# Turning Q, K and u by TensorE in all pairs and half batches instead of by the DMA crossbar

## The chip, the core and the metric

The kernel runs on one core of one Trainium2 chip. The metric is the device time of one execution in microseconds (us), and the figure given is the median of three runs. The five engines are TensorE (PE; its weight loads are listed apart as PEld), VectorE (DVE), ScalarE (ACT), GpSimd (POOL) and SyncE (SP). Each runs its own list of instructions in order, and they meet only at semaphores.

## The reference

The inputs are q, k and v for 4 batches, 8 heads, 768 positions and 64 channels per head. Block-sparse attention is followed by a mixer with four weight matrices:

```python
scores = scale * np.matmul(q, k.transpose(0, 1, 3, 2))
# blocks of 32: neighbours, first and last block, 3 sampled blocks per query block
scores = np.where(mask, scores, -1000000000.0)
scores = scores - np.max(scores, axis=-1, keepdims=True)
attn = np.exp(scores)
attn = attn / (np.sum(attn, axis=-1, keepdims=True) + 1e-09)
x = np.matmul(attn, v)                  # per head; then (B, S, H * D) = (4, 768, 512)
h = np.maximum(xt @ w_tok1, 0.0) @ w_tok2          # xt: (B, 512, 768); 768 -> 256 -> 768
u = x + h.transpose(0, 2, 1)
h2 = np.maximum(u @ w_ch1, 0.0) @ w_ch2            # 512 -> 1536 -> 512
return u + h2
```

All inner products run in bf16 with sums in float32; the output is float32.

## The kernel before

Two heads make a pair; there are 16 pairs (NP), four to a batch. Positions are spread over the 128 partitions in steps of six, so a head's 768 positions are six chunks (NC) of 128. A pair goes through these steps:

- Q, K and V are loaded by GpSimd's DMA queue (load_pair, L457), V is copied beside a column of ones (relayout, L790), and for pairs from 4 on Q and K are copied into the tiles klay and qlay, where one chunk holds both heads (relayout, L793).
- K and Q are turned, so that channels stand on the partitions: ktb and qtb, four buffers each (NV). This is the function transposes. Pairs 1 to 7 do it on TensorE against the identity (L882) with a copy out of PSUM (L895 or L911). Pairs from NPE = 8 on call crossbar, in which SP issues a DMA transpose each for K and for Q (L816).
- Scores (L941) are made in nine steps for a pair: three blocks t of 256 queries by three blocks jj of 256 keys. From pair 4 on the two heads use the two 64-row halves of the array at once. ScalarE takes the exp (L953), and from pair 4 on VectorE multiplies with a 0/1 mask (L970).
- P times V goes through L1082 (full height, 65 columns) for the first 18 blocks of queries, and from there on through the helper halves, whose matmuls all carry L386: a sum over 128 rows is cut into two sums over 64, which run side by side in the two halves of the array and end in two banks. VectorE divides by the sum (L1038 and L1039, or L1095 and L1096) and writes x.

When four pairs are done, the mixer of that batch begins. Its token part works on half batches (b, g), 256 channels each: tok for batches 1 to 3, tok_first on quarters for batch 0. It adds the result to x in place; this is u. Then u has to be turned for the channel part, into the tile uT, whose channels lie in four blocks of 128 (2 g + m). Batch 0 does this in turn_first (L1427), half batch (1, 1) in turn_by_pe (L1161, with copies L1172), and the other five, (1, 0), (2, 0), (2, 1), (3, 0) and (3, 1), in turn_by_crossbar (L1141, a DMA transpose from SP). The channel part ch multiplies with w_ch1 (L386 in halves, L1528 at full height for the last batch), takes the ReLU (L1124 on ScalarE, L1126 on VectorE), multiplies with w_ch2 (L386, L1593), adds u (L1559, L1607, L1615) and stores.

turn_by_pe and the half-height branch of transposes are built alike: six chunks, each with two matmuls of 64 rows by 64 columns, one per half of the array, in transpose mode, so 12 for one operand of a pair or one block of uT. The result fills two of the eight PSUM banks, and one copy of 128 x 768 by VectorE or ScalarE brings it to SBUF.

The order of the work is written out by hand at the top, as the dictionary ORDER: one string per engine, in which a letter names a stream and a number repeats it. On TensorE q is a score step, v and V are P times V, t the transposes of K and Q, f and g the token part of batch 0, k and K that of the others, c and C the channel part (capitals are the second halves), s and m the start. On ScalarE and VectorE e is an exp, x a masking, n a division, l and y the copies of Q, K and V, h the copy of turned K or Q, w that of turned u, r a ReLU, o an output. On SP b and u are the crossbar transfers. The class Planner follows these strings step by step with a cost for each operation, chooses PSUM banks and buffers by its own clock and emits the instructions. Its costs (RING, CLASH and the numbers at each P.op) decide banks and buffers, not the order.

The event all_loaded keeps the copies of K and Q for pairs from NPE on, and so their crossbar transfers, back until the last input load has landed. Between the first and second half of a sum in halves stands a fence: a no-op at L372 on SP, or on GpSimd once its loads are issued, for which the second half waits.

Of the kernel before, what the change touches and what calls it, by code (L numbers as in the profile page):

```python
# [28 lines left out]
def spell(text):  # L29

    steps = []
    for word in text.split():
# [7 lines left out]
        s q s q s t q s t3 q t2 q t v s v t v q t4 q v q2 v m v q2 v3 t3 q t3 q v q v t f2 t f6 t2 f4 t q v  # L40
        q2 t v2 q v2 f12 q t9 q f3 v f q v f t2 f t q t5 f t f q f8 q f2 q2 t5 v2 q v f2 v3 t f q f3 v q f4
        t2 f t f q v2 q f2 t2 f2 t f2 q2 v f v f t v f2 q f3 t2 f3 t q t2 f2 q v t v2 t q v3 t4 f q t6 g12
        q2 f5 g6 t f5 t5 f g6 q2 t f t4 v f t f4 g6 q v2 c3 q c3 q c2 C2 q C6 q v6 c5 q c5 q c C c q C7 q C4
        c6 q c2 C2 q C c4 q C6 c C c C2 c q v9 c q2 C2 k6 C2 K2 c3 q K c K3 q C4 v3 k v5 k v k2 c2 v2 c v K4
        c k V k c4 K V4 K V3 C4 V2 C q C2 V2 C c6 q v2 c2 v c q c v c v2 c q v6 C2 V4 q C V2 C V4 q C3 V2 C
        q C4 c q c3 q c2 q v2 c v3 c v c v c q v c v4 c q V6 C3 V v2 V v3 V v5 V2 v2 V C v3 C v V5 v V2 v2
        V2 v3 V3 v2 q C3 V12 C3 c v c q v2 C c v c2 v8 c q V12 c q c3 q k6 c q K c K5 q C2 v12 k3 V12 k q K4
        k2 C2 K2 q C2 q C2 k C k11 C3 c3 v2 c q v5 C3 v5 C c V c v2 V4 v c V c V2 v4 V2 v V2 v4 q C V12 C q
        C2 c5 q c5 C q c C2 q C5 c v12 C2 V5 q V C V5 C V c4 q c4 C c q c C c2 C v7 C v3 C v2 C2 q C V C V3
        C V8 C c C c3 v q v11 C2 V12 q C2 c2 q c2 k4 C k2 q C3 K2 v3 K v2 K v7 K2 c2 V c V11 c q c k4 c2 q c  # L50
        K4 C q C7 c3 k2 c q K c K q c4 q v2 c v8 c v2 q c V12 C q C3 v5 q v2 C2 v5 C q V2 C V9 q V C4 q c3 q
        c3 v q c v c2 v c v q v6 c v2 c v8 V4 C v2 V3 v4 C V4 v3 V4 v2 V C V2 v V2 v2 V3 v2 V C2 q V7 C V q
        V4 C5 k2 q k C k3 v12 K6 V5 q c2 V2 c V2 k3 V k V2 c k K4 k c2 q c K2 c3 q c2 q2 C5 q C7 q v24 V24 q
        c2 q c4 q C2 c C2 v12 c q V12 C2 q C2 q c10 C c v2 C2 v2 q c C3 v2 C v C2 v4 C v C2 V4 v V2 v V2 v V
        v3 V3 v6 q V12 q c3 q k6 c v4 K6 q C3 v8 C k4 V12 K q K3 c3 q c5 q C2 k2 C2 q K2 C4 c4 v12 q C V9 v
        V v V2 C v C2 v5 c2 v4 q c2 V10 q V2 C3 q C c10 C c q C4 c q C2 c2 C c2 q c3 v c v5 q v C2 v q v4 C3
        v V3 v2 V2 v V C V v4 V2 v2 V3 v2 c5 V v V C2 v c V c V3 v V v3 V2 v2 c V v V2 v3 C3 V12 c2 C c2 k12
        c4 k12 c6 C12 c194
    """),
    act=spell("""  # L60
        p e38 ag e2 h e6 r e r e4 r e3 r e3 r e3 r e13 l e8 w e r e6 r e2 r e r e2 l e2 r e3 r e14 l e11 r
        e4 r2 e4 r e4 r e3 r e6 ak
    """),
    dve=spell("""
        Z3 Y z5 H2 z n H2 Y S n m n H2 af Y n H2 n df2 H2 L2 n wf h H2 af l Y n h df n y df n h l wf n l Y h
        af l n l n x h l h df dg df dg x h wf wg n x4 n2 x3 r y x y x r x n3 x2 ak y r dk2 x n y x3 n x o l2
        x3 n l y x n2 x o l n x2 l ak x n dk2 x w x o x l2 n l n r x2 r n x4 n x y n r l x2 ak n l dk x2 dk
        x l n x3 n l o x2 y x n2 x n x o ak x n dk2 x l y x y x o n2 x3 n r x3 n2 x2 ak x n dk x dk x2 n r x
        n y x r x3 n x n2 o dk3 r o r13 o r2 o2 r o3 r o3
    """),  # L70
    sp=spell("""
        s2 b3 u b11 u b u b u2
# [39 lines left out]
RING = {"b": (1170.0, 1200.0, 1100.0), "u": (1170.0, 2200.0, 1400.0)}  # L112
CLASH = 3500.0
# [192 lines left out]
def kernel(  # L306
# [23 lines left out]
    NPE = 8  # L330
# [447 lines left out]
    copied, LAYS = {}, {}  # L778
    all_loaded = Ev()

    def relayout(p):
        lays = LAYS[p] = {}
        for nm in ("k", "q", "v") if p >= NT0 else ("v",):
# [3 lines left out]
            def emit(eng, nm=nm, raw=raw):  # L787
                copy = nc.scalar.copy if eng == "act" else nc.vector.tensor_copy
                if nm == "v":
                    copy(out=vaug[p % NV][:, :, :, 0:64], in_=raw)  # L790
                else:
                    lay = sbw.tile([128, NC, 2, D], BF16, tag=f"{nm}lay", bufs=2, name=f"{nm}lay{p}")
                    copy(  # L793
                        out=lay[:, :, :, :], in_=raw.rearrange("p h c d -> p c h d")
                    )
                    lays[nm] = lay
# [6 lines left out]
            if nm != "v" and p >= NPE:  # L803
                deps.append(all_loaded)
            lays[nm + "ev"] = P.op(("dve", "act") if p >= FORM["relay_act"] else ("dve",), {"dve": 290.0, "act": 660.0}, deps, emit,
# [5 lines left out]
    def crossbar(p):  # L811

        lays = LAYS[p]
        for nm, bufs, there in (("k", ktb, kT_there), ("q", qtb, qT_there)):
            def emit(eng, nm=nm, bufs=bufs):
                nc.sync.dma_start_transpose(  # L816
                    out=bufs[p % NV][:, 0, :].rearrange("e (c s) -> e c s", c=NC),
                    in_=lays[nm][:, :, :, :].rearrange("p c h d -> p (c h d)"),
                )
            deps = [lays[nm + "ev"], qk_done[p - NV]]  # L820
            ev = P.op(("sp",), {"sp": 1300.0}, deps, emit, lat=3500.0, label="b")
# [3 lines left out]
    def transposes(p):  # L825
        yield lambda: p in LAYS
        if p >= NPE:
            crossbar(p)
            return
# [88 lines left out]
    def alias(a, b):  # L918
        a.same_as = b
# [14 lines left out]
    def scores(s, bank, done, rel, exps):  # L934
# [3 lines left out]
        for i in range(2):  # L938
            for hd in range(2):
                rows, h = (slice(0, 88), hd) if p < NT0 else (slice(64 * hd, 64 * hd + 64), 0)  # L940
                nc.tensor.matmul(  # L941
                    out=ps[:, hd, 256 * i : 256 * i + 256],
                    lhsT=ktb[n][rows, h, 256 * jj + 128 * i : 256 * jj + 128 * i + 128],
                    rhs=qtb[n][rows, h, 256 * t : 256 * t + 256],
# [191 lines left out]
    def turn_by_crossbar(b, g, u_evs):  # L1136
        def emit(eng):
            if g == 0:
                new_uT(b)
                st[b]["uT_begun"].t = P.now  # L1140
            nc.sync.dma_start_transpose(  # L1141
                out=st[b]["uT"][:, g, :, :, :].rearrange("e c m p -> e (c m) p"),
                in_=st[b]["u"][:, g, :, :].rearrange("p c e -> p (c e)"),
            )

        begun = st[b].setdefault("uT_begun", Ev())
        ev = P.op(("sp",), {"sp": 1600.0}, u_evs + [begun] * (g == 1), emit, lat=3400.0, label="u",
                  tags=[("uT", 1)] if g == 0 else [])
        for dmc in (2 * g, 2 * g + 1):
            alias(st[b]["uT_there"][dmc], ev)  # L1150

    def turn_by_pe(b, g, u_evs):
        for m in range(2):
            last, rel, tbox = Ev(), Ev(), {}
            for sc in range(NC):
                def emit(sc=sc, m=m, rel=rel, tbox=tbox):
                    if sc == 0:
                        tbox["pt"] = P.bank("pm", 2, rel)
                    for row in range(2):
# [7 lines left out]
                yield 31.0, u_evs + [st[b]["uT_begun"]], [("pm", 2)] if sc == 0 else [], emit, last if sc == NC - 1 else None, 1  # L1167
# [13 lines left out]
    def tok(b, g):  # L1181
        deps = [x_there[2 * g + 4 * b + i, h] for i in range(2) for h in range(3)] + [tok1_there]
        if (b, g) not in FORM["tok_full"]:
            u_evs = yield from tok_halves(b, g, 0, 256, [deps] * NC, "k")
            if g == 1 and b in [1]:
                yield from turn_by_pe(b, g, u_evs)
            else:
                turn_by_crossbar(b, g, u_evs)
# [90 lines left out]
    def tok_full(b, g):  # L1279
# [47 lines left out]
        turn_by_crossbar(b, g, u_evs)  # L1327
# [429 lines left out]
```

## Time and profile before

| | |
|---|---|
| median of three runs | 243.68 us (243.25 to 243.77) |
| the profiled execution | 243.68 us, of which the span of instructions 241.5 us |
| TensorE matmuls busy | 236.4 us, 98% of the span, 4138 records |
| VectorE busy | 179.5 us, 74% |
| ScalarE busy | 163.0 us, 67% |
| GpSimd busy | 49.6 us, 21% |
| granted TensorE clock | 1.0 throughout |
| crossbar transfers | 8 for K, 8 for Q, 5 for u; first of K at 84.7 us, last of u at 201.4 us |

The span runs from the first to the last instruction on the chip. A row of a group of instructions gives line, engine, operation, tiles written and read, shape, count, then the busy time of all, the mean of one in ns, and the engine's idle time ahead of them. A row of the view by stretches gives, for each engine, busy time and number of instructions in that stretch, then the granted clock, the share of the DMA engines and their rate. A matmul's length in the records (190 to 380 ns) includes its way through the array, and the next one starts long before it ends; the distance of starts is the pace.

### The profile page before, as it was taken

The numbers are of one execution on the slowest core, as the hardware profiler recorded it, in microseconds if no ns is written. First come the engines' busy times: TensorE is split into PE (matmuls) and PEld (weight loads), VectorE is DVE, ScalarE is ACT, GpSimd is POOL, SyncE is SP. The second block draws the span as 40 slices with busy tenths as digits, with TensorE's granted clock in tenths as the row PEclk, the third lists the DMA queues.
The fourth block names the chain that finished last, engine by engine and source line by source line (L and its number), as shares of the span: only waits on it lengthen the run. The fifth ranks groups of instructions, "written<-read, shape, count | busy, mean of one in ns | idle before, by whom it ended". The sixth has DMA issues, their size and how long they took to land.

```text
span 241.5 us, 9252 instructions
## 1 busy us (share of the span) xinstructions
PE 236.4 (98%) x4138; PEld 171.8 (71%) x4138; DVE 179.5 (74%) x333; ACT 163.0 (67%) x175; POOL 49.6 (21%) x86
## 2 busy tenths in 40 slices
PE   7999999999999999999999999999999999999994
PEld 2699998866767576878888778678876664565443
DVE  5876977988878788887888788977795843587332
ACT  5999999999775977778989957788888500000000
POOL 8967896457610000000000000000000000000000
PEclk9999999999999999999999999999999999999999
DMA  7999999999990099674042183620030014011232
GB/s 163 163 204 212 208 208 203 206 201 203 199 190 10 3 156 203 87 111 79 3 57 46 37 168 109 125 97 3 4 58 15 0 67 90 30 57 46 88 126 92
DMA packets 39607, 26.12 MB, mean 108 GB/s; under 512 B 21968, under 2 KB 36960, under 8 KB 39568
## 3 DMA queue, kind: packets, MB, share of 16 engines
q0 software_dynamic: 15104, 12.98, 34.2%
q1 hardware_dynamic: 23920, 12.17, 22.8%
q8 instruction: 32, 0.52, 0.9%
q10 hardware_dynamic: 544, 0.39, 0.6%
q14 instruction: 7, 0.06, 0.1%
HBM read 26.74 MB, written 6.29 MB: 137 GB/s over the span
## 4 chain that ended last, share of the span: by engine, by line
PE 94%; DMA 2%; POOL 2%; issue 0%; DVE 0%; POOLq 0%
PE banks L386 52%; PE banks L941 16%; PE banks L1593 9%; PE banks L1528 6%; PE banks L1082 6%; DMA qraw<-in_q_dram 2%; PE banks L882 2%; PE banks L1348 1%; PE banks L1368 1%; PE banks L1290 1%; PE banks L1427 1%; PE banks L1310 1%; POOL ktb L529 0%; POOL ktb L533 0%; POOL vraw L457 0%; POOL kraw L457 0%
## 5 line engine op out<-in xcount | busy, mean ns | idle before, releaser
L953 ACT ACTIVATE et<-banks 128x1024 bf16<-128x1024 f32 x144 | 138.9, 1032 | 25.1 <-PE banks L941 24.2
L970 DVE TENSOR_TENSOR et<-et,mask 128x992 bf16<-128x992 bf16 x72 | 65.0, 928 | 5.2 <-ACT et L953 5.1
L941 PE MATMUL banks<-qtb,ktb 64*128 64x256 bf16 (+1 forms) x576 | 62.7, 270 | 0.2
L386 PE MATMUL banks<-uT,w_ch 64*128 64x256 bf16 (+1 forms) x576 | 61.8, 322 | 0.0
L386 PE MATMUL banks<-w_ch,rc 64*128 64x512 bf16 x384 | 55.0, 376 | 0.0
L386 PEld LDWEIGHTS <-et 64*128 64x128 bf16 x1440 | 37.9, 94 | 10.2 <-POOLq L372 1.0
L386 PE MATMUL banks<-vaug,et 64*128 64x65 bf16 x1440 | 43.6, 190 | 0.0
L941 PEld LDWEIGHTS <-ktb 64*128 64x128 bf16 (+1 forms) x576 | 33.9, 95 | 11.7 <-issue 0.4
L386 PEld LDWEIGHTS <-w_ch 64*128 64x128 bf16 x576 | 29.5, 94 | 7.9 <-POOLq L372 0.7
L1126 DVE TENSOR_SCALAR rc<-banks 128x512 bf16<-128x512 f32 (+1 forms) x27 | 23.1, 866 | 11.8 <-PE banks L1528 8.3
L386 PEld LDWEIGHTS <-rc 64*128 64x128 bf16 x384 | 19.0, 94 | 8.2 <-issue 0.4
L1593 PE MATMUL banks<-w_ch,rc 128*128 128x512 bf16 (+2 forms) x108 | 21.4, 355 | 0.0
L1124 ACT ACTIVATE rc<-banks 128x1024 bf16<-128x1024 f32 x18 | 18.4, 1027 | 0.7 <-PE banks L386 0.4
L1593 PEld LDWEIGHTS <-rc 128*128 128x128 bf16 x108 | 10.1, 98 | 10.5 <-issue 0.4
L1082 PE MATMUL banks<-vaug,et 128*128 128x65 bf16 x432 | 17.5, 193 | 0.0
L1082 PEld LDWEIGHTS <-et 128*128 128x128 bf16 x432 | 15.9, 97 | 1.3 <-issue 0.6
L1528 PE MATMUL banks<-uT,w_ch 128*128 128x512 bf16 (+1 forms) x96 | 15.8, 326 | 0.0
L1038 DVE RECIPROCAL recip<-banks 128x4 f32<-128x4 f32 x30 | 5.5, 182 | 13.5 <-PE banks L386 13.0
L386 PEld LDWEIGHTS <-w_tok 64*128 64x128 bf16 x240 | 13.1, 109 | 2.7 <-POOLq L372 0.3
L1528 PEld LDWEIGHTS <-w_ch 128*128 128x128 bf16 x96 | 9.4, 98 | 6.4
L1039 DVE TENSOR_TENSOR x<-banks,recip 128x256 bf16<-128x256 f32 x30 | 12.7, 424 | 1.0
L1607 DVE TENSOR_TENSOR o<-banks,x 128x512 f32<-128x512 f32 x7 | 4.8, 689 | 9.4 <-PE banks L1593 9.4
(113 smaller groups left out, 211.1 us busy)
## 6 DMA issues: line engine op xcount, KB each, us to landing
out_dram<-o SPq DMA_DIRECT2D x8, 512.0 KB, 2.9
w_ch<-in_moe_w_ch_dram POOLq DMA_DIRECT2D x8, 384.0 KB, 9.8
vraw<-in_v_dram POOLq DMA_DIRECT2D x10, 192.0 KB, 7.7
out_dram<-o SPq DMA_DIRECT2D x7, 256.0 KB, 2.0
kraw<-in_k_dram POOLq DMA_DIRECT2D x9, 192.0 KB, 8.5
qraw<-in_q_dram POOLq DMA_DIRECT2D x9, 192.0 KB, 7.9
w_tok<-in_moe_w_tok_dram POOLq DMA_DIRECT2D x2, 384.0 KB, 9.9
qf<-in_v_dram POOLq DMA_DIRECT2D x4, 192.0 KB, 7.7
```

Source lines behind the costliest of these rows:

```text
L386: mms.append(nc.tensor.matmul(out=outs()[o](x), lhsT=lhs(o, x, r), rhs=rhs(o, x, r), start=(back == 0 and x == 0), stop=(back == 1 and x = ...
L882: nc.tensor.matmul(out=box["t"][:, c, :], lhsT=rows, rhs=ident[:, :], start=(c == 0), stop=(c == NC - 1), is_transpose=True,)
L941: nc.tensor.matmul(out=ps[:, hd, 256 * i : 256 * i + 256], lhsT=ktb[n][rows, h, 256 * jj + 128 * i : 256 * jj + 128 * i + 128], rhs=qtb[n] ...
L953: nc.scalar.activation(out=ets[p, t][:, jj, :, :, :].rearrange("k i h q -> k h i q"), in_=ps.rearrange("k h (i q) -> k h i q", i=2), func= ...
L970: nc.vector.tensor_tensor(out=et, in0=et, in1=free(mask[:, 2 * lo, 256 * t + EDGE : 256 * t + EDGE + 1], 0, [[S, 2 * n], [0, 2], [1, w]]), ...
L1038: nc.vector.reciprocal(out=recip[:, :, :], in_=free(po, 64, [[512, 2], [65, 2]]))
L1039: nc.vector.tensor_tensor(out=free(xs[b][:, pb // 2, 2 * t, 128 * (pb % 2) : 128 * (pb % 2) + 128], 0, [[64, 2], [256, 2], [1, 64]],), in0 ...
L1082: nc.tensor.matmul(out=po[:, hd, c, :], lhsT=et[:, jj, i, hd, 128 * c : 128 * c + 128], rhs=va[:, hd, 2 * jj + i, 0:65], start=(jj == 0 an ...
L1124: nc.scalar.activation(out=o(), in_=src(), func=AF.Relu)
L1126: nc.vector.tensor_scalar(out=o(), in0=src(), scalar1=0.0, scalar2=None, op0=ALU.max)
L1528: nc.tensor.matmul(out=in_bank(pbox["pm"], [k, 128 * n])[:, x // 4, :], lhsT=w_ch1[:, x % 4, 128 * cc : 128 * cc + 128], rhs=st[b]["uT"][: ...
L1593: nc.tensor.matmul(out=pbox["pm"][:, 0:n], lhsT=box["rc"][:, cc, 128 * sc : 128 * sc + 128], rhs=w_ch2[:, cc, lo : lo + n], start=(cc == 0 ...
```

## The change

NPE goes from 8 to 16, the number of pairs. So pairs 8 to 15 take the half-height branch of transposes, and the branch for pairs from NPE on is reached by no pair. In its place the diff puts another function, through_dram, with a block transpose by VectorE, two staging tensors in DRAM and another layout of keys and queries in scores; all of it depends on p >= NPE. The wait for all_loaded is gone from relayout. turn_by_crossbar is gone, and tok and tok_full call turn_by_pe for all six half batches of batches 1 to 3; the first turned block of a batch now also takes the uT buffer. Batch 0 stays as it is. FORM is the same, ORDER is new for TensorE, ScalarE, VectorE and SP, where only the start's two entries are left. RING and CLASH have other values; after the change no operation uses RING's two entries. Line numbers move by some 14 to 33 places (L941 becomes L974, L1161 L1178, L1528 L1542, L1593 L1607).

```diff
--- before.py
+++ after.py
@@ -37,39 +37,39 @@
 
 ORDER = dict(
     pe=spell("""
-        s q s q s t q s t3 q t2 q t v s v t v q t4 q v q2 v m v q2 v3 t3 q t3 q v q v t f2 t f6 t2 f4 t q v
...
+        q s3 q s t6 q3 s q v t6 v2 q2 v2 t6 q t v t v t q t3 m q v2 q3 f v f5 v2 f2 q f3 v f q2 v2 q t4 f t
...
     act=spell("""
-        p e38 ag e2 h e6 r e r e4 r e3 r e3 r e3 r e13 l e8 w e r e6 r e2 r e r e2 l e2 r e3 r e14 l e11 r
...
+        p e37 h e ag e h e9 r e4 r e2 r e5 r l e4 w e3 h e10 h e2 h e l h e2 w e r e8 r e2 r e4 y ak e2 r e4
...
     sp=spell("""
-        s2 b3 u b11 u b u b u2
+        s2
     """),
 )
 AF = mybir.ActivationFunctionType
...
-RING = {"b": (1170.0, 1200.0, 1100.0), "u": (1170.0, 2200.0, 1400.0)}
-CLASH = 3500.0
+RING = {"b": (830.0, 1200.0, 1100.0), "u": (830.0, 1200.0, 1300.0)}
+CLASH = 2000.0
+TURN = 1050.0
...
     NET = 4
-    NPE = 8
+    NPE = 16
...
-                if nm == "v":
+                if nm != "v" and p >= NPE:
...
+                    lays[nm] = lay
+                elif nm == "v":
                     copy(out=vaug[p % NV][:, :, :, 0:64], in_=raw)
...
-            if nm != "v" and p >= NPE:
-                deps.append(all_loaded)
-            lays[nm + "ev"] = P.op(("dve", "act") if p >= FORM["relay_act"] else ("dve",), {"dve": 290.0, "act": 660.0}, deps, emit,
+            block = nm != "v" and p >= NPE
+            lays[nm + "ev"] = P.op(("dve", "act") if p >= FORM["relay_act"] and not block else ("dve",),
+                                  {"dve": TURN if block else 290.0, "act": 660.0}, deps, emit,
                                   label=("y" if nm == "v" else "l") if p >= FORM["relay_act"] else "Y" if nm == "v" else "L")
...
-    def crossbar(p):
+    def through_dram(p):
...
-                nc.sync.dma_start_transpose(
-                    out=bufs[p % NV][:, 0, :].rearrange("e (c s) -> e c s", c=NC),
-                    in_=lays[nm][:, :, :, :].rearrange("p c h d -> p (c h d)"),
+            where = stage[nm][p % 2]
...
+            put_ev = P.op(("sp",), {"sp": 500.0}, [lays[nm + "ev"]], put, lat=2500.0, label="b")
+            ev = P.op(("sp",), {"sp": 1500.0}, [put_ev, qk_done[p - NV]], get, lat=2500.0, label="u")
...
     def transposes(p):
         yield lambda: p in LAYS
         if p >= NPE:
-            crossbar(p)
+            through_dram(p)
...
+                keys = ktb[n][rows, h, 256 * jj + 128 * i : 256 * jj + 128 * i + 128]
+                rhs = qtb[n][rows, h, 256 * t : 256 * t + 256]
+                if p >= NPE:
+                    keys = ktb[n][rows, 0, :].rearrange("e (k c) -> e c k", c=NC)[:, 2 * jj + i, :]
+                    rhs = qtb[n][rows, 0, :].rearrange("e (b c j) -> e c b j", b=4, c=NC)[:, 2 * t : 2 * t + 2, :, :]
                 nc.tensor.matmul(
-                    out=ps[:, hd, 256 * i : 256 * i + 256],
-                    lhsT=ktb[n][rows, h, 256 * jj + 128 * i : 256 * jj + 128 * i + 128],
-                    rhs=qtb[n][rows, h, 256 * t : 256 * t + 256],
+                    out=ps[:, hd, 256 * i : 256 * i + 256], lhsT=keys, rhs=rhs,
...
-    def turn_by_crossbar(b, g, u_evs):
-        def emit(eng):
-            if g == 0:
-                new_uT(b)
-                st[b]["uT_begun"].t = P.now
-            nc.sync.dma_start_transpose(
-                out=st[b]["uT"][:, g, :, :, :].rearrange("e c m p -> e (c m) p"),
-                in_=st[b]["u"][:, g, :, :].rearrange("p c e -> p (c e)"),
-            )
-
-        begun = st[b].setdefault("uT_begun", Ev())
-        ev = P.op(("sp",), {"sp": 1600.0}, u_evs + [begun] * (g == 1), emit, lat=3400.0, label="u",
-                  tags=[("uT", 1)] if g == 0 else [])
-        for dmc in (2 * g, 2 * g + 1):
-            alias(st[b]["uT_there"][dmc], ev)
-
     def turn_by_pe(b, g, u_evs):
...
+                        if g == 0 and m == 0:
+                            new_uT(b)
...
-                yield 31.0, u_evs + [st[b]["uT_begun"]], [("pm", 2)] if sc == 0 else [], emit, last if sc == NC - 1 else None, 1
+                yield 31.0, u_evs, ([("pm", 2)] + [("uT", 1)] * (g == 0 and m == 0)) if sc == 0 else [], emit, last if sc == NC - 1 else None, 1
...
         if (b, g) not in FORM["tok_full"]:
             u_evs = yield from tok_halves(b, g, 0, 256, [deps] * NC, "k")
-            if g == 1 and b in [1]:
-                yield from turn_by_pe(b, g, u_evs)
-            else:
-                turn_by_crossbar(b, g, u_evs)
+            yield from turn_by_pe(b, g, u_evs)
...
-        turn_by_crossbar(b, g, u_evs)
+        yield from turn_by_pe(b, g, u_evs)
```

## The prediction

> **What bounds the kernel now.** I read the engines' totals and the chain that ended last first, then the stretches, then the waits. The page:
>
> ```profile
> span 241.5 us, 9252 instructions
> ...
> PE 236.4 (98%) x4138; PEld 171.8 (71%) x4138; DVE 179.5 (74%) x333; ACT 163.0 (67%) x175; POOL 49.6 (21%) x86
> ...
> PEclk9999999999999999999999999999999999999999
> ...
> PE 94%; DMA 2%; POOL 2%; issue 0%; DVE 0%; POOLq 0%
> ```
>
> TensorE is busy for 98% of the span, and 94% of the chain that ended last runs through it. A busy TensorE is not yet one at its pace, because matmuls overlap, so I add up the matmuls at the spacing that the timeline shows (start of one group to start of the next):
>
> - 336 pairs of 64x512 at 216 ns (ten rows in 1.08 us): 72.6
> - 480 pairs of 64x256 and 144 of 88x256 at 109: 68.0
> - 720 pairs of 64x65 at 30.4 (42 rows in 0.64 us): 21.9
> - 132 of 128x512 at 216, 72 of 128x256 at 109: 36.4
> - 432 of 128x65 at 29.6, about 228 of 128x128 at 56, the rest of small size: some 30
>
> That is 229 us of 241.5. Of the other 12.5, 1.0 lies before the first matmul and about 3 after the last (output add and store). Eighteen switches between full-height matmuls and pairs of 64 rows cost 0.1 to 0.2 each, some 2.2. Of the remaining 6, about 5 lie in the first 20 us, where starts are wider apart than the spacings above. The view by stretches says the same:
>
> ```profile
> core 0: us, PE busy (x) PEld busy (x) DVE busy (x) ACT busy (x) POOL busy (x), PEclk, DMA share, GB/s
> 0.00:20.00 20.00, 17.86 (x214) 12.80 (x215) 13.57 (x44) 16.14 (x20) 16.65 (x34) 1.00 1.03 182
> ...
> 100.00:120.00 20.00, 20.00 (x444) 16.29 (x442) 17.59 (x28) 16.59 (x18) 0.00 (x0) 1.00 0.35 59
> 120.00:140.00 20.00, 20.00 (x428) 16.05 (x422) 16.04 (x27) 18.79 (x21) 0.00 (x0) 1.00 0.26 42
> 140.00:160.00 20.00, 20.00 (x485) 15.45 (x482) 17.38 (x31) 13.78 (x16) 0.00 (x0) 1.00 0.64 143
> 160.00:180.00 20.00, 20.00 (x480) 15.87 (x478) 16.01 (x24) 18.26 (x20) 0.00 (x0) 1.00 0.06 16
> ```
>
> From 20 us on TensorE has no hole. The waits name who waits for whom (total us, times, longest), first the longest of all, then all of the matmuls' own and the longest of the weight loads:
>
> ```profile
> ACT et L953 <- PE banks L941: 24.2, 27, 3.5
> ...
> PE banks L522 <- DVE one L515: 1.0, 1, 1.0
> PE banks L597 <- ACT klay_first L589: 0.7, 2, 0.5
> PE banks L882 <- DMA qraw<-in_q_dram: 0.2, 1, 0.2
> ...
> PEld L386 <- POOLq L372: 2.1, 12, 0.2
> ```
>
> ScalarE waits for TensorE, not the other way round. TensorE's own waits are three at the start and the fences of L372, which hide beside running matmuls; none names a crossbar transfer, neither those that write ktb or qtb nor those that write uT. So each added TensorE nanosecond is a nanosecond of the end, and the crossbars hold nothing up.
>
> **What the change removes.** 21 crossbar transfers on SP's queue:
>
> ```profile
> ktb<-klay SPq DMA_TRANSPOSE x8, 4.6
> qtb<-qlay SPq DMA_TRANSPOSE x8, 3.5
> uT<-x SPq DMA_TRANSPOSE x5, 3.9
> ```
>
> With them go 21 issues on SP (1.2 to 1.5 us each) and their landing times, 3.5 to 4.6 us. As TensorE never waits for them, I count their removal as 0. At most a fence that SP holds for an L386 pair comes a little sooner; the wait list has 0.2 us in all for fences on SP. The copies of K and Q for pairs 8 to 15 no longer wait for the last input load; they move earlier on engines that wait for TensorE anyway: 0. Were the cover gone (TensorE short of work), a 4 us landing would show; here it never does. No load and no store is added on SP or GpSimd. The two DRAM staging tensors and the block transposes of the diff belong to pairs from NPE = 16 on, and there are 16 pairs, so none is issued.
>
> **What it adds on TensorE.** For each of 8 pairs, K and Q take 6 chunks by 2 row halves, 24 matmuls: 192. For five half batches of u, 2 by 6 by 2, 24 matmuls: 120. Sum 312, each with a weight load; the built program holds exactly these more and no other change on TensorE (4138 matmul records become some 4450). All stand among 64-row pairs, and the new order has 18 switches as before. Half batch (1, 1) already does it this way, so the trace has the row:
>
> ```profile
> 102.22 0.50 PE L1161 MATMUL banks<-ident,x 64*128 64x64 bf16 x21
> 102.54 0.38 PE L386 MATMUL banks<-w_ch,rc 64*128 64x512 bf16 x1
> ...
> L1161 PE MATMUL banks<-ident,x 64*128 64x64 bf16 x24 | 0.8, 190 | 0.0
> ```
>
> The 190 ns is one matmul's length; what counts is 0.32 us for 21 of them, or 22 if a record is missing: 14.5 to 15.2 ns each. 312 x 14.6 = 4.6 us (4.5 to 4.7).
>
> Two rules of the Trainium skill speak for a higher price. Its page "TensorE: Matmul & The Clock Gate", section "Wait — 56ns, not 53.3ns?", says that starts never come closer than about 25 ns however short the matmul; that makes 312 x 25 = 7.8 us and an end at 251.5. Here rows of 64 x 64 start 15 ns apart, two of them running in two halves of the array, so I take the row. Section "Part 4: PE-mode transpose" says transposes do not count as activity for the clock and cost about 275 ns in a kernel's context. If the clock fell to half for one window of 3.4 us (that page, Part 1) it would cost 1.7 us; but the stretch that holds these 24 transposes shows the granted clock at 1.00, and 0.8 us is all that a group has. I add nothing.
>
> **What it adds on the other engines.** 26 evacuations of 128x768 out of PSUM. The rows of the same shape:
>
> ```profile
> L1172 ACT COPY uT<-banks 128x768 bf16<-128x768 bf16 x1 | 0.8, 805 | 0.0
> L1172 DVE COPY uT<-banks 128x768 bf16<-128x768 bf16 x1 | 0.6, 553 | 0.0
> ```
>
> The new order puts 17 on VectorE (9.4 us) and 9 on ScalarE (7.2 us); some ReLUs and V copies change sides as well, about 1 us each way. The room from 60 to 200 us, by the stretches: VectorE idles 28 of 140 us, ScalarE 32. Both stay under 87% there, so this lies beside TensorE's work. Where cover is thin (ScalarE at 18.79 and 18.26 of 20), two more copies of 0.8 us in one stretch use it up; then the exps come late, and TensorE's next scores lack a bank.
>
> Latency: in the new order the transposes of K and Q stand at least 7 us of TensorE work ahead of the first scores that read them. For u the last chunk is needed soonest: 1.4 us after its transposes in batch 1, 1.1 us in batch 3 (between the end of the last transpose and the first L1542 matmul that reads it). Needed are about 0.2 drain (the 190 ns above), 0.55 to 0.8 copy and 0.1 to 0.2 of signals: 0.9 to 1.2 us. So it costs 0 to 0.3 at a few places.
>
> Banks: a transpose group holds two of eight banks for roughly 1.3 us (0.2 fill, 0.2 drain, copy, signals), 26 x 2 x 1.3 = 68 of some 1120 bank-us between 60 and 200 us. Bounds for the waits of the whole new order: -1.3 us (early holes that another order could close: some 2 us between 7 and 20 us are off pace, part of them at small mask matmuls that stay) to +2.5 us (each of the 26 groups late by 0.1). I take +0.1, near the row of now, where such waits are next to nothing from 20 us on.
>
> **Sum.** Profiled run 243.68 us, span 241.5; the 2.2 around the span stays. 241.5 + 4.6 + 0.1 = 246.2 span, 248.4 us. The profiled run equals the median of the three (243.68), so this is also the forecast for the median: +1.9%.
>
> **Rivals.**
> 1. TensorE begins to wait for evacuations or banks. For it: 16.6 us more on two engines that already run at 75 to 94% in places, and 26 more two-bank tenancies. Against: the slack above, and that 24 such transposes today cause no wait. At 0.1 to 0.15 us per group it adds 2.6 to 4: 250.9 to 252.3, say 251.2.
> 2. The short matmuls do not keep 15 ns apart when they come with other work between them (25 ns): 251.5. Against it the row shown, which is itself mixed with L386 matmuls.
> 3. Faster. One mechanism: the new order closes the start-up holes of the first 20 us, where TensorE is off pace by about 5 us. It would have to close over 4.6 us to decide, and at 5.0 the time would be 243.2. But more than half of these 5 us are the matmuls before the first scores (spacing 0.43 us instead of 0.216 for 128x512), whose code is unchanged; 1.3 us are left to win, so 247.1 is the likely limit.
> 4. The change does not do what it says: ruled out by the built program, which has no crossbar transfer.
>
> **How the numbers follow.** About 0.2% (0.5 us) can be told from no change here. Chances: forecast 0.77 (own range 247.3 to 249.7), rival 1 0.15, rival 2 0.05, rival 3 0.03. For 8 in 10 I leave out the top of rivals 1 and 2 and rival 3: 247.1 (holes closed) to 250.9 (rival 1 begins). Faster 0.03, within 0.2% 0.01, slower 0.96.
>
> **What would show it.** Right: some 4450 matmul records, PE again at about 98% with no DMA_TRANSPOSE, span near 246, groups of 64x64 rows 15 ns apart, stretches after 20 us still full, first L1542 matmul of batch 3 about 4.6 us later than the 207.2 of L1528 now. Wrong: waits of PE on the new copies or on exps of ScalarE (rival 1), 25 ns spacing or a granted clock below 1.00 (rival 2), a first 20 us with far more matmuls than 214 records (rival 3).

## The result, and the profile after

| | before | after |
|---|---|---|
| median of four runs | 243.47 us (243.04 to 243.77) | 249.5 us (249.32 to 249.75) |
| ratio | | 1.025, 95% interval 1.023 to 1.027 |
| profiled execution, span in it | 243.68, 241.5 us | 249.75, 248.0 us |
| first L1528 (after: L1542) matmul of the last batch | 207.17 us | 213.07 us |
| start of the last group of L1593 (L1607) matmuls | 222.77 us | 228.67 us |
| end of the last output add on VectorE | 238.83 us | 244.73 us |

The kernel is 6.0 us slower. Ranges and ratios, here and below, leave out single executions that the chip ran in a slower state. Between the sets of runs on different chips the kernel before has medians of 243.37 to 243.89 us, so a difference of less than about 0.5 us between two experiments says little by itself. From the last batch on all landmarks stand 5.90 us later in the profiled execution; the end behind the last add adds 0.2 (243.68 less 238.83 is 4.85, 249.75 less 244.73 is 5.02). The page of the kernel after, its totals and the chain that ended last:

```profile
span 248.0 us, 9867 instructions
...
PE 241.2 (97%) x4446; PEld 175.2 (71%) x4450; DVE 187.6 (76%) x346; ACT 172.3 (69%) x188; POOL 49.6 (20%) x86
...
PE 85%; DMA 5%; POOL 5%; DVE 3%; issue 1%; DVEq 0%; POOLq 0%
```

The 4450 weight loads are those forecast. What is new is the chain: of the 94% on TensorE 9 points have gone to DMA, GpSimd and VectorE. The early part of the chain runs over the load of a K tile (landed at 24.65 us) and then along VectorE to 32.3 us. The view by stretches (busy time and number for each engine, granted clock, DMA share and rate) says where TensorE is short of work:

```profile
core 0: us, PE busy (x) PEld busy (x) DVE busy (x) ACT busy (x) POOL busy (x), PEclk, DMA share, GB/s
0.00:20.00 20.00, 18.09 (x222) 12.96 (x223) 14.81 (x48) 16.61 (x20) 15.44 (x33) 1.00 1.01 183
20.00:40.00 20.00, 18.98 (x329) 17.77 (x327) 15.91 (x38) 18.60 (x21) 17.06 (x31) 1.00 1.22 206
...
120.00:140.00 20.00, 20.00 (x494) 15.76 (x492) 16.21 (x27) 18.70 (x21) 0.00 (x0) 1.00 0.01 4
```

From 40 to 200 us the stretches are full at clock 1.00, as forecast; from 200 to 220 us they show 19.79, because one matmul record of L1607 is missing there (two weight loads at 212.63, one matmul). Between 20 and 40 us 1.0 us is missing, and 329 matmuls stand where there were 349. The longest waits of TensorE for other engines (total us, times, longest):

```profile
PE banks L523 <- DVE one L516: 1.0, 1, 1.0
PE banks L974 <- DVE x L1127: 0.9, 1, 0.9
PE banks L613 <- DVE qtb L606: 0.4, 1, 0.4
```

The first and third belong to the start. The second is new: one score step waits for one division on VectorE. None names a new copy out of PSUM (L886, L1189). The new transposes themselves, on TensorE's timeline:

```profile
105.43 0.34 PE L1178 MATMUL banks<-ident,x 64*128 64x64 bf16 x12
105.61 0.60 PE L387 MATMUL banks<-w_ch,rc 64*128 64x512 bf16 x4
```

Twelve take 0.18 us from start to next start, 15 ns each. The copies behind them:

```profile
L886 DVE COPY ktb<-banks 128x768 bf16<-128x768 bf16 x7 | 3.9, 556 | 1.3 <-PE banks L875 1.0 <-ACT et L984 0.2
L886 ACT COPY qtb<-banks 128x768 bf16<-128x768 bf16 x5 | 4.0, 799 | 0.7 <-PE banks L875 0.6
L1189 DVE COPY uT<-banks 128x768 bf16<-128x768 bf16 x9 | 5.0, 557 | 2.7 <-PE banks L1178 2.5
```

556 and 799 ns are the 553 and 805 of the old rows. Now the hole. TensorE between 25.7 and 32.8 us (start, us until the last end, line, tiles, shape, count, idle before):

```profile
25.77 0.41 PE L1113 MATMUL banks<-vaug,et 128*128 128x65 bf16 x8
26.34 0.38 PE L910 MATMUL banks<-ident,klay 128*128 128x128 bf16 x4 [0.16 <-DVE x L1127]
...
30.82 0.65 PE L1113 MATMUL banks<-vaug,et 128*128 128x65 bf16 x16
32.33 0.60 PE L974 MATMUL banks<-qtb,ktb 88*128 88x256 bf16 x4 [0.86 <-DVE x L1127]
```

At 29.6 ns each, eight P times V matmuls from 25.77 end their turn at 26.01, and the next group starts 0.33 later; sixteen from 30.82 end theirs at 31.29, and the scores start 1.04 later. Together 1.4 us. No new transpose lies before 78 us, so this is none of their doing. What VectorE did meanwhile:

```profile
28.28 0.47 DVE L811 COPY qlay<-qraw 128x768 bf16<-128x768 bf16 x1
28.68 0.54 DVE L1455 COPY uT<-banks 128x768 bf16<-128x768 bf16 x1
29.14 1.42 DVE L808 COPY vaug<-vraw 128x768 bf16<-128x768 bf16 x2
30.48 0.80 DVE L811 COPY klay<-kraw 128x768 bf16<-128x768 bf16 x1
31.20 0.54 DVE L811 COPY qlay<-qraw 128x768 bf16<-128x768 bf16 x1
31.66 0.16 DVE L1126 RECIPROCAL recip<-banks 128x4 f32<-128x4 f32 x1
31.85 0.42 DVE L1127 TENSOR_TENSOR x<-banks,recip 128x256 bf16<-128x256 f32 x1
```

The division at 31.66 frees the bank of a P times V unit whose matmuls had ended at 29.3. Ahead of it in VectorE's list stand six copies without a pause, 3.4 us: three of K or Q, two of V, one of turned u. The order before has a division, a ReLU and a division among such copies, and no matmul waits for them:

```profile
26.52 0.18 DVE L1095 RECIPROCAL recip<-banks 128x4 f32<-128x4 f32 x1
...
29.16 0.42 DVE L1126 TENSOR_SCALAR a_t<-banks 128x256 bf16<-128x256 f32 x1
29.50 0.79 DVE L793 COPY klay<-kraw 128x768 bf16<-128x768 bf16 x1
30.21 0.79 DVE L790 COPY vaug<-vraw 128x768 bf16<-128x768 bf16 x1
31.34 0.18 DVE L1095 RECIPROCAL recip<-banks 128x4 f32<-128x4 f32 x1 [0.34 <-PE banks L1082]
```

Single copies are about as long there (0.79 us), so their length is not new; their place is. The first hole, 0.33 us, has a second cause. Its division stands behind a copy of K that VectorE has to wait 0.31 us for, because the load has only just landed; in the order before this copy starts at 25.68 and waits for nothing.

```profile
24.67 0.36 DVE L811 COPY klay<-kraw 128x768 bf16<-128x768 bf16 x1 [0.31 <-DMA kraw<-in_k_dram]
...
25.64 0.18 DVE L1126 RECIPROCAL recip<-banks 128x4 f32<-128x4 f32 x1
```

So the 6.07 us between the two profiled executions is 312 x 14.6 ns = 4.55, holes 1.35 to 1.4, end 0.2; all else is nothing on balance.

### The profile page after: what moved, and what is told of

Its sections match the earlier page's. It is cut to its first block, busy times and chain, and to the rows that moved or that the text cites. A ratio compares the mean times of both kernels' runs of the same rounds, so it can differ in the third digit from the quotient of the medians.

```text
span 248.0 us, 9867 instructions
## 1 busy us (share of the span) xinstructions
PE 241.2 (97%) x4446; PEld 175.2 (71%) x4450; DVE 187.6 (76%) x346; ACT 172.3 (69%) x188; POOL 49.6 (20%) x86
## 4 chain that ended last, share of the span: by engine, by line
PE 85%; DMA 5%; POOL 5%; DVE 3%; issue 1%; DVEq 0%; POOLq 0%
PE banks L387 50%; PE banks L974 12%; PE banks L1607 8%; PE banks L1542 6%; DMA kraw<-in_k_dram 5%; PE banks L1113 3%; POOL vraw L458 1%; PE banks L875 1%; PE banks L1382 1%; PE banks L910 1%; POOL kraw L458 1%; POOL qraw L458 1%; PE banks L1178 1%; DVE vaug L808 1%; PE banks L1362 1%
## 5 line engine op out<-in xcount | busy, mean ns | idle before, releaser
L974 PE MATMUL banks<-qtb,ktb 64*128 64x256 bf16 (+1 forms) x576 | 62.4, 270 | 1.1 <-DVE x L1127 0.9
L387 PE MATMUL banks<-uT,w_ch 64*128 64x256 bf16 (+1 forms) x576 | 59.7, 322 | 0.0
L387 PE MATMUL banks<-w_ch,rc 64*128 64x512 bf16 x384 | 55.6, 376 | 0.0
L974 PEld LDWEIGHTS <-ktb 64*128 64x128 bf16 (+1 forms) x576 | 32.5, 95 | 14.4 <-issue 1.8
L387 PEld LDWEIGHTS <-et 64*128 64x128 bf16 x1440 | 35.0, 94 | 7.8 <-POOLq L373 0.5
L387 PE MATMUL banks<-vaug,et 64*128 64x65 bf16 x1440 | 40.3, 190 | 0.0
L387 PEld LDWEIGHTS <-w_ch 64*128 64x128 bf16 x576 | 28.0, 94 | 8.9 <-POOLq L373 0.2
L1157 DVE TENSOR_SCALAR rc<-banks 128x512 bf16<-128x512 f32 (+1 forms) x27 | 24.1, 906 | 7.3 <-PE banks L1542 3.9
L1155 ACT ACTIVATE rc<-banks 128x1024 bf16<-128x1024 f32 (+1 forms) x18 | 17.5, 976 | 8.1 <-PE banks L1542 7.4
L387 PEld LDWEIGHTS <-rc 64*128 64x128 bf16 x384 | 18.2, 94 | 6.6 <-issue 0.4
L1607 PE MATMUL banks<-w_ch,rc 128*128 128x512 bf16 (+2 forms) x104 | 21.9, 355 | 0.3 <-issue 0.2
L1113 PEld LDWEIGHTS <-et 128*128 128x128 bf16 x432 | 16.4, 97 | 0.9 <-issue 0.4
L1607 PEld LDWEIGHTS <-rc 128*128 128x128 bf16 x108 | 10.0, 98 | 9.9 <-issue 0.4
L1542 PE MATMUL banks<-uT,w_ch 128*128 128x512 bf16 (+1 forms) x96 | 15.8, 326 | 0.0
L1542 PEld LDWEIGHTS <-w_ch 128*128 128x128 bf16 x96 | 9.4, 98 | 6.4
```

What stands on the lines that cost most here:

```text
L387: mms.append(nc.tensor.matmul(out=outs()[o](x), lhsT=lhs(o, x, r), rhs=rhs(o, x, r), start=(back == 0 and x == 0), stop=(back == 1 and x = ...
L974: nc.tensor.matmul(out=ps[:, hd, 256 * i : 256 * i + 256], lhsT=keys, rhs=rhs, start=(i == 0), stop=(i == 1),)
L1113: nc.tensor.matmul(out=po[:, hd, c, :], lhsT=et[:, jj, i, hd, 128 * c : 128 * c + 128], rhs=va[:, hd, 2 * jj + i, 0:65], start=(jj == 0 an ...
L1155: nc.scalar.activation(out=o(), in_=src(), func=AF.Relu)
L1157: nc.vector.tensor_scalar(out=o(), in0=src(), scalar1=0.0, scalar2=None, op0=ALU.max)
L1542: nc.tensor.matmul(out=in_bank(pbox["pm"], [k, 128 * n])[:, x // 4, :], lhsT=w_ch1[:, x % 4, 128 * cc : 128 * cc + 128], rhs=st[b]["uT"][: ...
```

## The experiments

**The changed kernel again** (no edit), for the spread between executions.

> The changed kernel as it is, on the chip of the runs beside it: 249.5 us, 1.025 of the kernel before. It is the base for the next three.

249.58 us (249.02 to 249.64), ratio 1.0239 (1.0211 to 1.0266). Its profiled execution was the 249.02. In it the first hole is gone (the copy of K starts at 24.47 and does not wait), the second is 0.34 us instead of 1.04, and the last group of L1607 starts at 227.85, 0.82 earlier. The copies in front of the division were shorter this time (350 ns for a copy of V where the other execution has 673). So the size of the second hole varies from one execution to the next, with the length of the copies ahead of it.

**One division moved forward.** The first reading was that a single division stands too late.

```diff
-        ... h L wf Y2 l2 n y af n h df2 n h n l
+        ... h L wf n Y2 l2 y af n h df2 n h n l
```

> The changed kernel, but on VectorE the division that stands behind two copies of V and two of K and Q (at 31.7 us in the trace) goes ahead of the four. Theory A: what the change costs over the 4.6 us of its transposes, some 1.4 us, is VectorE's queue between 24 and 32 us: TensorE waits 1.0 us at 31.3 us for a bank which that late division frees. Then 248.5 us, and the hole of 1.0 us is gone. Rival B: the 1.4 us are small waits at the 26 new copies out of PSUM, 0.05 us each: 249.5. Rival C: the holes come from the late load of K of pair 4 (landed at 24.7 us), whatever the order: 249.5.

249.91 us, 1.0252 (1.0224 to 1.028): a miss. TensorE's timeline shows the hole at the scores closed and a new one behind it:

```profile
31.03 0.60 PE L974 MATMUL banks<-qtb,ktb 88*128 88x256 bf16 x4
31.47 0.28 PE L910 MATMUL banks<-ident,qlay 128*128 128x128 bf16 x2
33.08 0.55 PE L1382 MATMUL banks<-a_t,w_tok 128*128 128x128 bf16 x7 [1.33 <-DVE a_t L1157]
```

The ReLU (af in the string) stands behind the same copies in both orders, and is now the first to be missed. Not one division is late: the train of copies stands ahead of all that TensorE needs next. The theory became that.

**The train broken up.** The divisions and the ReLU go ahead of copies whose readers come later.

```diff
-        ... h L wf Y2 l2 n y af n h df2 n h n l
+        ... h L wf n Y l af l n h df2 Y n y h n l
```

> The changed kernel with VectorE's train of copies at 28 to 32 us pulled apart: two of the V copies go some 4 us later, behind copies and adds that TensorE waits for, and the division and the ReLU of the token part come earlier. All the work stays. Division_first closed the hole at the bank and opened one of 1.5 us at that ReLU, so theory A now reads: it is VectorE's queue as a whole that is late there, and what does not press must move out of it. Then no hole over 0.3 us between 24 and 34 us, and 248.7 us (249.58 less 0.9). Rival C (late loads, or a lack that only moves on): another hole opens behind it and the time stays at 249.5.

248.65 us (248.44 to 249.14), 1.0193 (1.0153 to 1.0232): as the theory of VectorE's order has it. The scores follow on time (sixteen at 29.6 ns are 0.47), and the stretch is full again:

```profile
30.56 0.65 PE L1113 MATMUL banks<-vaug,et 128*128 128x65 bf16 x16
31.04 0.60 PE L974 MATMUL banks<-qtb,ktb 88*128 88x256 bf16 x4
```

```profile
20.00:40.00 20.00, 19.93 (x347) 18.70 (x346) 15.69 (x40) 19.74 (x22) 16.60 (x30) 1.00 1.23 206
```

The last group of L1607 starts at 227.39, 4.62 us after the kernel before: the price of 312 transposes and next to nothing else, which leaves nothing for the other values of RING and CLASH and the banks chosen by them. The intervals of this ratio and of the changed kernel's overlap, so it is the profile that decides. A hole of 0.24 us is left at 25.8, where VectorE waits 0.22 us for the same load of K; in this small part rival C was right.

**GpSimd's mask copies moved ahead.** Why is the train so long? A copy of 128x768 from SBUF takes 350 ns at best and up to 830 here, and GpSimd spreads the mask in the same stretch (its copies at L760, 26.4 to 29.0 and 31.1 to 33.7 us). The edit puts all of them behind the loads of pair 4 and ahead of those of pairs 5 and 6.

```diff
-        if NT0 <= p <= NT0 + 2:
-            loads.append(spread_mask(p - NT0))
+        if p == NT0:
+            loads += [spread_mask(0), spread_mask(1), spread_mask(2)]
```

> The changed kernel with GpSimd's three groups of mask copies one after the other, ahead of the loads of pairs 5 and 6. In the trace VectorE's copies of 128x768 take 450 to 830 ns between 28 and 32.7 us instead of 350. If the mask copies of GpSimd slow them, these copies come down to 350 there, VectorE's queue is 1.5 us shorter, the hole at 31.3 us closes and the time is 248.5 us. If the writing of load descriptors slows them, or nothing of GpSimd does, they stay at 450 to 830 and the time is 249.5. Later loads (by up to 5 us) could cost something instead: then over 249.5.

251.79 us, 1.0339 (1.0307 to 1.0371): slower. VectorE's timeline:

```profile
29.30 0.63 DVE L808 COPY vaug<-vraw 128x768 bf16<-128x768 bf16 x2
29.84 0.34 DVE L811 COPY klay<-kraw 128x768 bf16<-128x768 bf16 x1
31.50 0.41 DVE L811 COPY qlay<-qraw 128x768 bf16<-128x768 bf16 x1 [1.32 <-DMA qraw<-in_q_dram]
...
41.68 0.36 DVE L811 COPY klay<-klay_first 128x768 bf16<-128x768 bf16 x1 [2.16 <-DMA klay_first<-in_k_dram]
```

Half of the expectation held: the copies came down to 340 to 411 ns. But the loads queued behind the masks on GpSimd land later, and VectorE waits 1.3 and 2.2 us for them. This shows that GpSimd's work in this stretch lengthens the train, though not which part of it, since the issues of loads moved as well. It is no cure.

**All added transposes twice.** TensorE does each of the 312 a second time, into the same place.

```diff
-                        for row in range(2):
+                        for row in (0, 1) * (1 + (p >= 8)):
...
-                    for row in range(2):
+                    for row in (0, 1) * (1 + ((b, g) != (1, 1))):
```

> Each of the 312 added 64x64 transposes is done twice into the same place, the copies out of PSUM stay as they are. Theory A: 312 x 14.6 ns = 4.6 us more than the changed kernel's 249.6, so 254.1. With a floor of 25 ns a matmul: 257.4. If part of the transposes stood in gaps of TensorE that are free anyway: under 253.

253.99 us, 1.0409 (1.0359 to 1.0459). 4.4 us more than the changed kernel (249.58), for 312: 14.1 ns each. The two sets ran on different chips, so this is uncertain by a ns or two; in the profile 24 transposes from 80.46 us take 0.35 us to the next start, 14.6 ns each. This measures the disputed price by itself, and the 25 ns between starts of rival 2 are not there for these pairs in two halves.

**Full height instead of halves.** With tr_full the transposes of pairs 8 to 15 go 128x128 through the whole array: 96 at 56 ns (5.4 us) instead of 192 at 14.6 (2.8), and the array changes between full height and halves around them.

```diff
-    tr_full=7,
+    tr_full=15,
```

> The 192 added transposes of K and Q as 96 of 128x128 at full height instead of pairs of 64 rows. By pace 96 x 56 - 192 x 14.6 = 2.6 us more. They also stand among 64-row matmuls, so TensorE switches 86 times instead of 18; at 0.12 us each 8.2 us more. Theory A: 249.6 + 10.8 = 260.4. If a switch costs only where TensorE's queue runs empty: about 252.2.

259.11 us, 1.0622 (1.0571 to 1.0674): 9.5 us more. TensorE's timeline around one group:

```profile
87.65 0.81 PE L387 MATMUL banks<-w_ch,rc 64*128 64x512 bf16 x6
88.40 0.51 PE L910 MATMUL banks<-ident,klay 128*128 128x128 bf16 x6
88.84 0.39 PE L974 MATMUL banks<-qtb,ktb 64*128 64x256 bf16 x4
```

Six rows of 64x512 at 108 are 0.65, the next group starts after 0.75; six transposes at 56 are 0.34, the next starts after 0.44. That is 0.10 us a switch; by the whole, (9.5 - 2.6) us over the 68 switches that are new (86 instead of 18) is 0.10 too. The forecast needs none of these, since its transposes stand among 64-row pairs; had they been full height, it would have missed by more than the change costs.

**All added copies twice.** Each of the 26 evacuations of L886 and L1189 is done a second time: 16.4 us more, 18 x 0.555 on VectorE and 8 x 0.805 on ScalarE (the expectation has 17 and 9).

```diff
-                    copy(
-                        out=buf[:, 0, :]...
+                    for _ in range(2):
+                        copy(
+                            out=buf[:, 0, :]...
...
-                copy(
-                    out=st[b]["uT"][:, g, :, m, :]...
+                for _ in range(1 + ((b, g) != (1, 1))):
+                    copy(
+                        out=st[b]["uT"][:, g, :, m, :]...
```

> Each of the 26 added copies of 128x768 out of PSUM is done twice, on the engine that has it (17 on VectorE, 9 on ScalarE, 16.6 us of work more). Theory A: they lie beside TensorE's work, so within 0.8 us of the changed kernel: 249.5 to 250.3. Rival B, the copies and the banks that they hold cost 0.05 us each already: 2 us more or above, 251.5 to 254.

258.74 us, 1.0606 (1.0545 to 1.0666): 9.2 us more, a miss for both. Matmuls wait, and for the copies:

```profile
PE banks L975 <- ACT qtb L887: 1.0, 3, 0.5
PE banks L975 <- DVE ktb L887: 0.7, 2, 0.5
PE banks L387 <- DVE ktb L887: 0.7, 3, 0.3
```

A second copy lengthens two things, the engines' work and the time that two banks are held. The next run parts them.

**Spare work.** After each added copy, three copies of 128x256 in SBUF on VectorE, or two on ScalarE, into a tile that nobody reads. They hold no bank.

```diff
+    spare = {e: sb1.tile([128, 256], BF16, name=f"spare_{e}") for e in ("act", "dve")}
...
+                    for _ in range(2 if eng == "act" else 3):
+                        copy(out=spare[eng][:, :], in_=mask[:, 0, 0:256])
```

> Copies_twice cost 9 us for 16.6 us of work, so the room beside TensorE is smaller than reckoned. Here each of the 26 added copies is followed by work on the same engine that reads no PSUM bank and that nobody waits for: three copies of 128x256 in SBUF on VectorE, two on ScalarE, by the sum some 0.5 and 0.7 us each, 15 us in all. Theory D: what copies_twice paid for is the two banks that each copy holds longer, while TensorE's order counts on them: then 249.6 to 251.5 us here. Theory E: it paid for the engines' time, which the masks, exps and divisions behind it then lack: 255 to 258.

255.92 us, 1.0494 (1.0466 to 1.0521): 6.3 us more for 18.7 us of work (54 x 0.224 on VectorE, 16 x 0.41 on ScalarE; the two largest groups are shown), a third of a us for each.

```profile
L892 DVE COPY spare_dve<-mask 128x256 bf16<-128x256 bf16 x30 | 6.7, 224 | 0.7
L892 ACT COPY spare_act<-mask 128x256 bf16<-128x256 bf16 x12 | 4.9, 409 | 0.2
```

```profile
PE banks L977 <- ACT et L987: 1.4, 3, 0.5
PE banks L977 <- DVE x L1130: 1.0, 1, 1.0
PE banks L387 <- DVE o L1579: 0.7, 2, 0.4
```

The second line is the hole at 31 us, which stands ahead of all spare work. In the main it is the engines' time that counts: exps and outputs behind the spare work come late. Scaled to the 16.4 us of the run before, 6.3 x 16.4 / 18.7 = 5.5 of its 9.2 us would be the engines' time and 3.7 the banks held; that split is an estimate.

**Half of each copy.** The 16 copies of K and Q bring only half of their columns, and so leave half of ktb and qtb as it was.

```diff
-                        out=buf[:, 0, :].rearrange("e (c u s) -> e c u s", c=NC, u=2),
-                        in_=free(t, 0, [[64, NC], [1024, 2], [1, 64]]),
+                        out=buf[:, 0, :].rearrange("e (c u s) -> e c u s", c=NC, u=2)[:, 0 : NC // 2],
+                        in_=free(t, 0, [[64, NC // 2], [1024, 2], [1, 64]]),
```

> The 16 added copies for K and Q of pairs 8 to 15 bring only half of their columns (128x384 instead of 128x768; the rest of ktb and qtb stays as an earlier pair left it). Theory A, single copies are covered: no change, 249.3 to 249.7 us. If the copies already cost at their present length (as rival B says, 0.05 us each, or part of the 9 us of copies_twice): 248.8 or less.

249.78 us, 1.025 (1.022 to 1.0279): nothing gained. The single copies of K and Q are covered as they stand, and nothing is left for rival 1 there. The ten copies of u were not shortened; for them only the profile after speaks, in which no matmul waits on L1189.

**K and Q by the crossbar again**, u by TensorE, in the new order (without its t after pair 7 and its 16 h). The wait for all_loaded is left out, as in the changed kernel. RING and CLASH, by which banks are chosen, go back to their values before.

```diff
-        s2
+        s2 b16
...
-    NPE = 16
+    NPE = 8
...
-    def through_dram(p):
+    def crossbar(p):
...
+                nc.sync.dma_start_transpose(
+                    out=bufs[p % NV][:, 0, :].rearrange("e (c s) -> e c s", c=NC),
+                    in_=lays[nm][:, :, :, :].rearrange("p c h d -> p (c h d)"),
                 )
...
+            deps = [lays[nm + "ev"], qk_done[p - NV]]
```

> One part alone: u is turned by TensorE as in the change, K and Q of pairs 8 to 15 by the crossbar as before (192 matmuls and 16 copies out of PSUM less, 16 DMA transposes more, the orders otherwise those of the change). Theory A, crossbars and copies free, 14.6 ns a matmul: 249.5 - 192 x 0.0146 = 246.7 us. Rival B, each copy costs 0.05 us too: 245.9. If the crossbars' landing or SP's queue holds TensorE up: over 247.5.

247.67 us, 1.0184 (1.0145 to 1.0223): 1.9 less than the changed kernel, where 192 transposes are 2.8. SP's issues and TensorE's weight loads on the timeline:

```profile
60.98 2.25 SPq L833 DMA_TRANSPOSE qtb<-qlay  x1
63.34 1.20 PEld L386 LDWEIGHTS <-w_ch 64*128 64x128 bf16 x22 [0.38 <-SPq L372]
...
68.63 1.23 SPq L833 DMA_TRANSPOSE ktb<-klay  x1
69.97 0.10 PEld L386 LDWEIGHTS <-w_tok 64*128 64x128 bf16 x2 [0.64 <-SPq L372]
```

The fence of L372 stands on SP behind a transfer that takes 1.2 to 2.3 us to issue, and the second half of a sum waits for the fence: 1.2 us in three places in all, where the changed kernel has 0.3.

**The same with the wait for all_loaded**, as in the kernel before.

```diff
-            deps = [lays[nm + "ev"], qk_done[p - NV]]
+            deps = [lays[nm + "ev"], qk_done[p - NV], all_loaded]
```

> Kq_crossbar once more (K and Q of pairs 8 to 15 by the crossbar, u by TensorE), with its DMA transposes held back until the last input load has landed, as in the kernel before. In kq_crossbar TensorE waited 0.4 and 0.6 us at 63 and 70 us for fences that stood behind crossbar issues of 1.2 to 2.3 us on SP's queue. If these two waits are all that lay between its 247.67 us and the 246.7 reckoned, it is 246.6 to 246.9 us now. If the crossbars cost elsewhere: 247.4 or more.

246.94 us, 1.0128 (1.0107 to 1.0149), 0.7 less, though the two intervals touch. In the profile of the next run, which keeps the wait, TensorE's weight loads wait 0.3 us for SP's fences instead of 1.2. The wait that looked like a brake keeps crossbar issues off SP while SP carries the fences; GpSimd takes these over once its loads are issued.

**Both together**: crossbars for K and Q with that wait, and the train broken up.

> Kq_crossbar_late together with the order of VectorE of copies_apart: K and Q by the crossbar, u by TensorE, no train of copies. If the parts add up: 248.65 - 192 x 0.0146 = 245.85 us. What is then left over the kernel before (243.5) is 120 transposes of u, 1.75 us, and some 0.5. If the late K and Q of the crossbar need the slack that the train of copies took: over 246.5.

246.13 us (245.97 to 246.37), 1.01 (1.0081 to 1.012): 0.3 above the sum of the parts. Over the kernel before (243.75 beside it) that is 2.4 us, of which 120 transposes of u are 1.75; no version tried here beats the kernel before.

## Why the prediction was right, and where it failed

Direction, size and bound were right: 248.4 forecast, 249.5 measured, inside the range of 247.1 to 250.9. Two of its own signs did not come: the stretch from 20 to 40 us is not full, and the first matmul of the last batch stands 5.90 us later instead of 4.6. By its steps:

- **TensorE is the bound, each added ns is one of the end.** Right. Doubling the 312 moves the end by 4.4 us, and with the train broken up the last group of L1607 stands 4.62 late where 4.55 was reckoned.
- **14.6 ns a transpose.** Right: 15 in the row, 14.1 in the doubling. Rival 2, 25 ns spacing, falls with it. By an estimate from the 25 ns of the section "Wait — 56ns, not 53.3ns?" on the Trainium skill's page "TensorE: Matmul & The Clock Gate" the doubling would have added 7.8 us; for pairs in two halves of the array the measurement decides. The clock stayed at 1.00 in the stretches that hold the transposes.
- **Removal of the crossbars counted as 0.** Right: with K and Q back on the crossbar and the wait kept, 246.94 is 2.6 under the changed kernel, and the 192 transposes alone are 2.8. The five transfers of u were not put back by themselves. An issue on SP took 1.2 to 2.7 us in the kernel before, not 1.2 to 1.5. The term for fences on SP, "at most 0.2", was right only for the place where the crossbars stood before; issued earlier they cost about 0.7.
- **Evacuations hidden.** Right in the sum as far as tested, since halving the K and Q copies gains nothing. The new copies are 18 on VectorE and 8 on ScalarE, 16.4 us, instead of 17 and 9. The argument for it was wrong. I counted idle time from 60 to 200 us (28 us on VectorE, 32 on ScalarE) as room for the copies, and by that count as much again would have been free. It cost 6.3 us as spare work and 9.2 as second copies. Idle time in a sum is not room in the places where work falls.
- **Latency of u and of K and Q, 0 to 0.3.** No wait of a matmul on L886 or L1189 shows; nothing to be seen of it.
- **Waits of the new order, +0.1.** This is the step that failed: about +1.35 in the profiled execution, inside its bounds of -1.3 to +2.5, and with the end behind the last add (0.2, in no term) it is the whole miss. That the time still fell into the range owes something to luck: the room upward had been left for the 26 new groups, and something else used it. The prediction gave this term "near the row of now", from the full stretches after 20 us of the order before. But the orders of all engines were new from the first letter on, and I had looked for what the transposes meet, so after 60 us and at the end. The loss lies at 24 to 33 us, in VectorE's string, where copies were put together ahead of a division and a ReLU, and a copy of K ahead of another division before its load had landed. It could have been seen in the code: between "wf" and "n" stand Y2 l2, four copies at 350 ns or more each, and the bank that this n frees is wanted by the scores.
- **Rival 3** (start-up holes closed) did not show as a gain: the first 20 us hold 222 matmul records against 214, far from what it needed.

Left open: which share of the 9.2 us of second copies is bank holding, and why the second hole is 1.04 us in one execution and 0.34 in another. That it goes with the copies' length is seen in both traces, but what sets their length in one execution was not tried by itself.

## What to carry to other kernels

When an order is rewritten everywhere, its price has to be looked for everywhere: follow each engine's new list from its start, and ask of every run of copies what stands behind it and which bank or operand that frees. The price of an added instruction on the bounding engine is the distance of starts in a row of the same form and the same array mode; 64x64 pairs among 64-row work cost 14 to 15 ns each, and a detour through another mode costs more than the work. Test cover by adding spare work, not by adding up idle time: here 16.4 us fitted, and 18.7 more cost a third of their length.

## What was not expected of the hardware

- The same copy of 128x768 in SBUF on VectorE takes 350 ns or up to 830, while GpSimd works. Between 28 and 33 us it took 450 to 540 in the changed kernel beside the mask copies and up to 830 beside the issues of loads between them; with the mask copies moved away it took 340 to 411, though issues ran beside them too. The kernel before has two of 0.79 us there. The section "Who interferes with whom" of the Trainium skill's page "SBUF — State Buffer" says that a VectorE copy in a mode that uses two ports and a GpSimd instruction lock each other out for a whole instruction. That copies grow beside GpSimd's work agrees in kind; that these copies run in such a mode, and which instruction held up which copy, no run here shows.
- A change of the array between full height and halves costs 0.10 us, so the 68 new ones of the full-height run, 6.9 us, cost more than the 96 transposes that they surrounded (5.4).
- One crossbar transfer occupies SP's issue for 1.2 to 2.7 us (kernel before), and in the run with K and Q by the crossbar a no-op behind it held TensorE's weight loads by 0.4 and 0.6 us.
